# Attention and a gated MLP on one core: the softmax sums are kept, judged on the chip, and a second path stands behind a branch of GpSimd

## The chip, the cores and the metric

The kernel runs on one core of a Trainium2 chip. The core has a matrix engine (TensorE, PE in the profile, with its weight loads PEld), a vector engine (VectorE, DVE), a scalar engine (ScalarE, ACT), GpSimd (POOL) and SyncE (SP), which issues most transfers. The metric is the time of one execution on the device in microseconds (us); less is better. The kernel before takes 237.99 us, the median of three runs (237.53 to 238.32).

## What is computed

Eight batches, 384 tokens, 16 query heads on 4 key heads of 64 columns, a model width of 1024 and a gated MLP with 512 gated columns. Inputs and output are float32. Cut to what matters:

```python
scores = scale * np.matmul(q, k.transpose(0, 1, 3, 2))       # scale = 1/8
scores = scores - np.max(scores, axis=-1, keepdims=True)
attn = np.exp(scores)
attn = attn / (np.sum(attn, axis=-1, keepdims=True) + 1e-09)
x = np.matmul(attn, v)            # heads side by side: (8, 384, 1024)

h = np.maximum(x @ w_in, 0.0)     # (8, 384, 1024)
u, v = h[..., :512], h[..., 512:]
v_n = (v - mu) / np.sqrt(var + 1e-06)            # over the 512 columns
v_s = einsum('ts,bsd->btd', w_spatial, v_n) + b_spatial[None, :, None]
out = (u * v_s) @ w_out
```

The draws are small: `q`, `k` and `v` have a standard deviation of 0.1, so a score times its scale has one of about 0.01, each exponential is close to 1, and the sum of a query's 384 exponentials is close to 384.

## The kernel before

All matrix products are in float16 with float32 sums. The order of every engine's instructions is written out by hand: the kernel switches the scheduler off (line 51), and what the program issues first stands first in that engine's queue. A small planner in the kernel keeps a model clock of TensorE, ACT and DVE; `bank` (line 77) gives each product one of the eight PSUM banks, the one that by this model comes free first, and `spend` and `reads` (lines 85 and 88) advance the clock.

The attention of a batch is cut into 6 sets (3 tiles of 128 queries, 2 pairs of key heads). `units` (line 264) makes the scores, `exp` (line 288) the exponentials on ACT, with no maximum taken off first. `weigh` (line 292) multiplies them by the values. The values carry a column of ones, so each head's 65th column is the sum of its exponentials. DVE takes the reciprocal of four such columns into a small tile `r`, from a pool of four buffers (line 309), and multiplies by it:

```python
r = small.tile([P, G, 1], FP32, name=f"r_{b}_{s}_{hh}", tag="r")
reads(dve, 600.0, f"av_{b}_{s}_{hh}")
dve.reciprocal(r, o[:, :, D : D + 1])
```

That is done 96 times (8 batches, 6 sets, 2 halves), so 384 columns of `r` are made in all, and each is dead after its multiplication.

The MLP of a batch is a generator, `gated` (line 487), from which the attention's loop draws pieces of TensorE work. Of batch b it yields: `v_part` for three tiles of tokens (line 346; DVE takes the ReLU and the statistics), `u_part` for four blocks of columns (line 407; ReLU on ACT), and in the midst of these `root` (line 382, ACT) and `norm` (line 389: DVE makes `nmr`, POOL the three normalised tiles `vn`). Then, for each of four blocks, one output product of the batch before (`o_part`, line 456) and `s_part` (line 426: the product over tokens, then on DVE the sum `vs` with the bias, then on POOL the gate `gT`). The outputs of batch 7 come last, six calls of `o_part`, each copied by DVE or ACT and sent by SP or ACT. By then all attention is long done.

A program begins with a barrier of all engines that POOL opens, after four small memsets of constants; the profile has them at line 786. It ends with SP waiting for the transfers and engines one after the other, and two more barriers that POOL opens (line 797).

Of the kernel before, what the change touches and what calls it, by code (L numbers as in the profile page):

```python
# [1 line left out]

# [6 lines left out]

FP32 = mybir.dt.float32  # L10
FP16 = mybir.dt.float16
AF = mybir.ActivationFunctionType
ALU = mybir.AluOpType
PSUM = bass.MemoryType.PSUM
# [3 lines left out]
def kernel(  # L18
# [14 lines left out]
    nc = tc.nc  # L33
    P = 128
    B, HQ, S, D = q.shape
    HKV = k.shape[1]
    DM = moe_w_in.shape[0]
    DFF = moe_w_in.shape[1]
    DH = DFF // 2
# [3 lines left out]
    G = HQ // HKV  # L43
# [3 lines left out]
    SETS = 2 * NT  # L47
    UNITS = NT * SETS
    STEPS = UNITS // 2

    ctx.enter_context(tc.manual_schedule())

    cst = ctx.enter_context(tc.tile_pool(name="cst", bufs=1))
    ld = ctx.enter_context(tc.tile_pool(name="ld", bufs=2))
    att = ctx.enter_context(tc.tile_pool(name="att", bufs=2))
    moe = ctx.enter_context(tc.tile_pool(name="moe", bufs=2))
    small = ctx.enter_context(tc.tile_pool(name="small", bufs=4))
    ops = ctx.enter_context(tc.tile_pool(name="ops", bufs=3))
    ps = ctx.enter_context(tc.tile_pool(name="ps", bufs=1, space=PSUM))

    need = {AF.Exp, AF.Relu, AF.Copy, AF.Ln}
    set_id = next(
# [4 lines left out]
            name=nc.get_next_instruction_name(), act_func_set_id=set_id, ins=[], outs=[]  # L67
        )
    )
    pool, dve, act, sp = nc.gpsimd, nc.vector, nc.scalar, nc.sync  # L70
# [6 lines left out]
    def bank(shape, dtype, name):  # L77
        i = min(range(8), key=done.__getitem__)
        t = ps.tile(shape, dtype, name=name, tag=f"bank{i}")
        clock[nc.tensor] = max(clock[nc.tensor], done[i])  # L80
        done[i] = 1e12 + clock[nc.tensor]
        taken[name] = i
        return t

    def spend(ns):
        clock[nc.tensor] += ns

    def reads(eng, ns, name=None):
        clock[eng] = max(clock[eng], clock[nc.tensor] + 200.0) + ns
        if name:  # L90
            done[taken.pop(name)] = clock[eng]

    C512, C384, C128 = 216, 162, 56

    zero16 = cst.tile([P, P], FP16, name="zero16")
    dve.memset(zero16, 0.0)
# [54 lines left out]

    w_in16 = cst.tile([P, NK, DFF], FP16, name="w_in16")
    w_out16 = cst.tile([P, NM, DM], FP16, name="w_out16")
    wsT16 = cst.tile([P, NT, S], FP16, name="wsT16")
    bias_bc = cst.tile([P, S], FP32, name="bias_bc")
# [14 lines left out]

    ident16 = cst.tile([P, P], FP16, name="ident16")
    make_identity(nc, ident16)
    v1 = [cst.tile([P, HKV, NT, VW], FP16, name=f"v1_{i}") for i in range(2)]
    for i in range(2):
# [85 lines left out]


    aTs, x16s, xts = {}, {}, {}

    def units(u, count):
        b, r = divmod(u, UNITS)
        s, kt0 = divmod(r, NT)
        qt, j = divmod(s, 2)
        kts = range(kt0, kt0 + count)
        if kt0 == 0:
            aTs[b, s] = att.tile([P, NT, 2, G * P], FP16, name=f"aT_{b}_{s}", tag="aT", bufs=3)  # L270
        scs = [
            (kt, hh, bank([P, G * P], FP32, f"sc_{b}_{s}_{hh}_{kt}"))
            for hh in range(2)
            for kt in kts
        ]
        for kt, hh, sc in sorted(scs, key=lambda x: x[:2]):
            rows = slice(hh * D, (hh + 1) * D)
            nc.tensor.matmul(  # L278
                sc,
                kTs[b][rows, j, kt * P : (kt + 1) * P],  # L280
                qTs[b, j][rows, qt].rearrange("p (r i c) -> p i r c", r=G, i=G),
                start=True,
                stop=True,
            )
        spend(count * C512 + 186)
        return [(aTs[b, s][:, kt, hh], sc, f"sc_{b}_{s}_{hh}_{kt}") for kt, hh, sc in scs]

    def exp(a, sc, name):
        reads(act, 480.0, name)
        act.activation(a, sc, AF.Exp, scale=scale)  # L290

    def weigh(b, s, hh):
        qt, j = divmod(s, 2)
        aT = aTs[b, s]
        av = bank([P, 512], FP32, f"av_{b}_{s}_{hh}")
        for kt in range(NT):
            for i in range(G):
                nc.tensor.matmul(  # L298
                    av[:, i * (D + 1) : (i + 1) * (D + 1)],
                    aT[:, kt, hh, i * P : (i + 1) * P],  # L300
                    v1[b % 2][:, 2 * j + hh, kt, 0 : D + 1],
                    start=(kt == 0 and i == 0),
                    stop=(kt == NT - 1 and i == G - 1),
                )
        if s == 0 and hh == 0:
            x16s[b] = att.tile([P, NT, DM], FP16, name=f"x16_{b}", tag="x16")
        o = av[:, 0 : G * (D + 1)].rearrange("p (i d) -> p i d", i=G)
        spend(372)
        r = small.tile([P, G, 1], FP32, name=f"r_{b}_{s}_{hh}", tag="r")
        reads(dve, 600.0, f"av_{b}_{s}_{hh}")  # L310
        dve.reciprocal(r, o[:, :, D : D + 1])  # L311
        c = j * 512 + hh * 256
        dve.tensor_tensor(  # L313
            x16s[b][:, qt, c : c + 256].rearrange("p (i d) -> p i d", i=G),
            o[:, :, 0:D],
            r.to_broadcast([P, G, D]),
            ALU.mult,
        )
        measure()
# [62 lines left out]
    def root(b):  # L382
        measure()
        rstd = small.tile([P, NT], FP32, name=f"rstd_{b}", tag="rstd")
        act.activation(rstd, mvs[b][:, :, 1], AF.Ln, bias=eps_t)
        act.activation(rstd, rstd, AF.Exp, scale=-0.5)
        mvs[b, "rstd"] = rstd

    def norm(b):
        rstd = mvs[b, "rstd"]  # L390
        nmr = small.tile([P, NT], FP32, name=f"nmr_{b}", tag="nmr")
        dve.scalar_tensor_tensor(  # L392
            nmr, mvs[b][:, :, 0], -1.0, rstd, op0=ALU.mult, op1=ALU.mult
        )
        for st in range(NT):
            vn = moe.tile([P, DH], FP16, name=f"vn_{b}_{st}", tag="vn", bufs=6)
            (dve if b == 0 and st == 1 else pool).tensor_scalar(  # L397
                vn,
                v_r.pop((b, st)),
                rstd[:, st : st + 1],  # L400
                nmr[:, st : st + 1],
                op0=ALU.mult,
                op1=ALU.add,
            )
            v_n[b, st] = vn

    def u_part(b, m):
        if m == 0:
# [13 lines left out]
        reads(act, 400.0, f"pu_{b}_{m}")  # L422
        act.activation(uTs[b][:, m, :], pu[:, 0:S], AF.Relu)  # L423
        yield C384
# [62 lines left out]
    def gated():  # L487
        for b in range(B):
            u0 = b * UNITS
            behind = [(b - 1, tt, half) for tt in range(NT) for half in range(2)] if b else []  # L490
            if b == 0:
                for st in range(NT):
                    yield ("from", 6 * st + 7)
                    yield from v_part(b, st, 0, 4)
                    yield ("from", 6 * st + 10)
                    yield from v_part(b, st, 4, 8)
            else:
                yield ("from", u0 + 12)
                yield from v_part(b, 0)
                for _ in range(1 if b == B - 1 else 2):  # L500
                    yield from o_part(*behind.pop(0))
                yield ("from", u0 + 18)
                yield from v_part(b, 1)
                yield ("from", u0 + 24)
                yield from v_part(b, 2)
            for m in range(NM):
                i = 0
                for x in u_part(b, m):
                    yield x
                    i += 1  # L510
                    if (m, i) == (1, 6):
                        root(b)
                    if (m, i) == (2, 3):
                        norm(b)
            for m in range(NM):
                if behind:
                    yield from o_part(*behind.pop(0))
                yield from s_part(b, m)
            if behind:
                yield from o_part(*behind.pop(0))  # L520
        for tt in range(NT):
            for half in range(2):
                yield from o_part(B - 1, tt, half)
# [165 lines left out]
    total = UNITS * B  # L689
    ends = {}  # L690
    for i in range(SETS * B):
        ends.setdefault(NT * i + 4, []).append(divmod(i, SETS))
    fill = gated()
    wait_for = [0]

# [73 lines left out]
    wait_for[0] = 0  # L769
    pour(10**6, 1e12)  # L770
    assert not todo and not ends and next(fill, None) is None, (todo, ends)


# [28 lines left out]
```

## Time and profile before

| | us |
|---|---|
| median of three runs (lowest, highest) | 237.99 (237.53, 238.32) |
| span of the profiled execution | 236.4 (236.36 with one more digit) |
| median less span | 1.63 |
| busy in the span: PE, ACT, DVE, POOL | 230.1, 169.5, 142.7, 101.5 |
| PE busy between 216 and 231.8 us | all of it |

The span runs from the first instruction to the last of one profiled execution, so the metric holds a little more than it. An engine's busy time says how long instructions of its own ran. "Idle before" is time in which the engine stood still ahead of an instruction, and the arrow names what ended that wait. The granted TensorE clock is full (1.000) over the whole span. A row of the timeline is: start, duration, engine, line, operation, output and inputs, shape, count, and the idle time before it in brackets.

### The profile page before, as it was taken

The page shows a single profiled execution, that of the slowest core. Times are in us where ns is not written, and L with a number is a line of the kernel's source. Part 1 is how long each engine was busy: PE and PEld are TensorE (multiplying, and loading weights), DVE is VectorE, ACT ScalarE, POOL GpSimd, SP SyncE. Part 2 cuts the span into 40 slices and gives each one's busy share as a digit, 9 for nine tenths or more (in the row PEclk, how much of TensorE's full clock was granted, in tenths as well). Part 3 has the DMA queues.
Part 4 walks back from the last instruction along what each step waited for, and adds up shares of the span by engine and source line. Part 5 has one row for each costly group of instructions (what it writes and reads, how often), then busy time and mean ns, then how long its engine had stood idle before and what let it go on. Part 6 is the DMA issues. An engine that isn't in the chain of part 4 may idle for free.

```text
span 236.4 us, 5917 instructions
## 1 busy us (share of the span) xinstructions
PE 230.1 (97%) x2312; PEld 123.6 (52%) x2312; DVE 142.7 (60%) x379; ACT 169.5 (72%) x348; POOL 101.5 (43%) x145
## 2 busy tenths in 40 slices
PE   7899999999999999999999999999999999999993
PEld 6455655545554546544564545555465455545541
DVE  2568774676457764566646576376744667367362
ACT  2999989969997869977797776986697776401211
POOL 3669583651464543275045800575022500460550
PEclk9999999999999999999999999999999999999999
DMA  6999979999998999899989899389912643240147
GB/s 196 273 305 320 272 143 178 212 266 260 259 227 208 260 372 192 228 200 318 193 239 224 234 202 302 63 281 158 257 26 44 114 155 89 49 177 0 68 200 267
DMA packets 67467, 47.47 MB, mean 201 GB/s; under 512 B 48336, under 2 KB 60416, under 8 KB 67440
## 3 DMA queue, kind: packets, MB, share of 16 engines
q1 hardware_dynamic: 62512, 39.86, 69.4%
q0 software_dynamic: 3952, 6.42, 12.2%
q10 hardware_dynamic: 976, 0.82, 1.1%
q8 instruction: 18, 0.29, 0.5%
q14 instruction: 9, 0.07, 0.1%
HBM read 25.95 MB, written 12.58 MB: 163 GB/s over the span
## 4 chain that ended last, share of the span: by engine, by line
PE 93%; DVE 2%; DMA 2%; issue 0%; ACTq 0%; ACT 0%
PE pu L412 18%; PE pv L353 18%; PE po L469 18%; PE sc L278 15%; PE av L298 15%; PE psp L431 7%; DMA q<-in_q_dram 2%; PE qps L238 1%; PE xps L330 1%; DVE x L313 1%; DVE osb L216 1%; DVE qT L216 0%; DVE q L206 0%; DVE r L311 0%; DVE vr L367 0%
## 5 line engine op out<-in xcount | busy, mean ns | idle before, releaser
L290 ACT ACTIVATE aT<-sc 128x512 f16<-128x512 f32 x288 | 147.7, 612 | 31.0 <-PE sc L278 30.3
L298 PEld LDWEIGHTS <-aT 128*128 128x128 f16 x1152 | 47.0, 97 | 17.0 <-issue 2.1
L353 PE MATMUL pv<-w_in,xt 128*128 128x512 f16 x192 | 51.0, 380 | 0.1
L298 PE MATMUL av<-v,aT 128*128 128x65 f16 x1152 | 50.5, 193 | 0.0
L469 PE MATMUL po<-w_out,gT 128*128 128x512 f16 (+2 forms) x196 | 50.5, 375 | 0.0
L412 PE MATMUL pu<-xt,w_in 128*128 128x384 f16 x256 | 49.9, 326 | 0.0
L397 POOL TENSOR_SCALAR vn<-vr,rstd,nmr 128x512 f16<-128x512 f32 x23 | 17.7, 783 | 66.7 <-DVE nmr L392 45.3
L448 POOL TENSOR_TENSOR gT<-vs,uT 128x384 f16<-128x384 f32 x31 | 32.5, 1058 | 31.8 <-DVE r L311 16.9
L313 DVE TENSOR_TENSOR x<-av,r 128x256 f16<-128x256 f32 x96 | 40.7, 424 | 3.3
L278 PE MATMUL sc<-qT,kT 64*128 64x512 f16 x288 | 41.6, 380 | 0.4 <-DVE qT L216 0.2
L311 DVE RECIPROCAL r<-av 128x4 f32<-128x4 f32 x96 | 17.1, 179 | 40.4 <-PE av L298 40.1
L216 DVE COPY osb<-po 128x512 f32<-128x512 f32 (+1 forms) x39 | 26.6, 683 | 17.3 <-PE po L469 17.2
L412 PEld LDWEIGHTS <-w_in 128*128 128x128 f16 x256 | 22.1, 98 | 17.1 <-issue 5.5
L423 ACT ACTIVATE uT<-pu 128x384 f16<-128x384 f32 x32 | 15.8, 495 | 16.0 <-PE pu L412 15.8
L469 PEld LDWEIGHTS <-gT 128*128 128x128 f16 x196 | 17.4, 98 | 17.3 <-issue 3.2
L353 PEld LDWEIGHTS <-xt 128*128 128x128 f16 x192 | 15.8, 97 | 17.8 <-issue 6.0
L278 PEld LDWEIGHTS <-kT 64*128 64x128 f16 x288 | 10.9, 94 | 23.7 <-issue 12.1
L431 PE MATMUL psp<-wsT,vn 128*128 128x384 f16 x96 | 22.2, 327 | 0.0
L443 DVE TENSOR_TENSOR vs<-psp,bias_bc 128x384 f32<-128x384 f32 x32 | 17.6, 552 | 7.0 <-PE psp L431 6.9
L201 POOL CAST q<-q 128x768 f16<-128x768 f32 x22 | 17.6, 831 | 9.2 <-DMA q<-in_q_dram 4.5
L367 DVE TENSOR_SCALAR vr<-pv 128x512 f32<-128x512 f32 x24 | 16.4, 683 | 8.4 <-PE pv L353 8.3
L379 DVE BATCH_NORM_STATS2 stats<-vr 128x6 f32<-128x512 f32 x24 | 16.4, 685 | 0.1
(47 smaller groups left out, 98.9 us busy)
## 6 DMA issues: line engine op xcount, KB each, us to landing
out_dram<-osb SPq DMA_DIRECT2D x21, 512.0 KB, 3.2
q<-in_q_dram SPq DMA_DIRECT2D x10, 768.0 KB, 5.8
v_None<-in_v_dram SPq DMA_DIRECT2D x6, 384.0 KB, 5.8
w_in<-in_moe_w_in_dram POOLq DMA_DIRECT2D x4, 512.0 KB, 9.8
k_None<-in_k_dram SPq DMA_DIRECT2D x5, 384.0 KB, 4.0
q<-in_q_dram POOLq DMA_DIRECT2D x2, 768.0 KB, 8.4
out_dram<-osb SPq DMA_DIRECT2D x5, 256.0 KB, 2.2
w_out<-in_moe_w_out_dram POOLq DMA_DIRECT2D x2, 512.0 KB, 8.5
```

The lines of the kernel that those rows point to most:

```text
L201: eng.tensor_copy(t16[:, :, :, hh, :], src[:, hh])
L216: (act.copy if eng is act else dve.tensor_copy)(o, i)
L278: nc.tensor.matmul(sc, kTs[b][rows, j, kt * P : (kt + 1) * P], qTs[b, j][rows, qt].rearrange("p (r i c) -> p i r c", r=G, i=G), start=True ...
L290: act.activation(a, sc, AF.Exp, scale=scale)
L298: nc.tensor.matmul(av[:, i * (D + 1) : (i + 1) * (D + 1)], aT[:, kt, hh, i * P : (i + 1) * P], v1[b % 2][:, 2 * j + hh, kt, 0 : D + 1], st ...
L313: dve.tensor_tensor(x16s[b][:, qt, c : c + 256].rearrange("p (i d) -> p i d", i=G), o[:, :, 0:D], r.to_broadcast([P, G, D]), ALU.mult,)
L353: nc.tensor.matmul(pv, xts[b][:, kt, st * P : (st + 1) * P], w_in16[:, kt, DH:DFF], start=(kt == 0), stop=(kt == NK - 1),)
L397: (dve if b == 0 and st == 1 else pool).tensor_scalar(vn, v_r.pop((b, st)), rstd[:, st : st + 1], nmr[:, st : st + 1], op0=ALU.mult, op1=A ...
L412: nc.tensor.matmul(pu[:, 0:S], w_in16[:, kt, m * P : (m + 1) * P], xts[b][:, kt, :], start=(kt == 0), stop=(kt == NK - 1),)
L431: nc.tensor.matmul(psp[:, 0:S], v_n[b, st][:, m * P : (m + 1) * P], wsT16[:, st, :], start=(st == 0), stop=(st == NT - 1),)
L448: pool.tensor_tensor(gT, vs, uT, ALU.mult)
L469: nc.tensor.matmul(po[:, 0:width], gTs[b][:, m, tt * P : (tt + 1) * P], w_out16[:, m, c0 : c0 + width], start=(m == 0), stop=(m == NM - 1),)
```

## The change

The 96 small tiles `r` become slices of one tile `r_all` of 128 x 384 in the constant pool. It is never reused, so at the end it holds every reciprocal.

`judge` is called once, in the last batch, while `u_part` of its third block is under way. DVE reduces `r_all` over its 384 columns three times (maximum, minimum, sum). POOL fills `ones16` (128 x 128) and makes from the three values, in three instructions on 128 x 1, a float16 flag per partition: 1 if the minimum is above 0, the maximum at most 1 and the sum above 0, else 0.

`count` is called once, ahead of the third of the four last `s_part` blocks. TensorE multiplies the flags by the ones (one weight load and one product of one column, in a PSUM bank of its own), which gives the number of good partitions, and ACT copies it to SBUF.

After all else POOL loads that number into a register and compares it with the bits of 128.0. If it is another, POOL alone runs `with_maximum`, which computes the whole result again in float32, with each query's maximum, in loops, one instruction at a time, and overwrites the output. If it is 128.0, POOL jumps over that code. The other engines have no branch; SP waits for one more semaphore, which POOL sets on either way, before the last barriers. The code that is jumped over has some 1,020 instructions of POOL. In the built program four instructions that set registers of POOL also stand ahead of its four first memsets, before the opening barrier.

```diff
-    ctx.enter_context(tc.manual_schedule())
+    order = ctx.enter_context(ExitStack())
+    order.enter_context(tc.manual_schedule())
...
+    r_all = cst.tile([P, B * SETS * 2 * G], FP32, name="r_all")
...
-        r = small.tile([P, G, 1], FP32, name=f"r_{b}_{s}_{hh}", tag="r")
+        n = (b * SETS + s) * 2 + hh
+        r = r_all[:, n * G : (n + 1) * G].rearrange("p (i a) -> p i a", a=1)
...
+    ext = cst.tile([P, 3], FP32, name="ext")
+    fine16 = cst.tile([P, 1], FP16, name="fine16")
+    ones16 = cst.tile([P, P], FP16, name="ones16")
+    count32 = cst.tile([P, 1], FP32, name="count32")
+
+    def judge():
+        for i, op in enumerate((ALU.max, ALU.min, ALU.add)):
+            dve.tensor_reduce(ext[:, i : i + 1], r_all, axis=mybir.AxisListType.X, op=op)
+        pool.memset(ones16, 1.0)
+        pool.tensor_scalar(ext[:, 1:2], ext[:, 1:2], 0.0, None, op0=ALU.is_gt)
+        pool.tensor_scalar(ext[:, 0:1], ext[:, 0:1], 1.0, ext[:, 1:2], op0=ALU.is_le, op1=ALU.mult)
+        pool.tensor_scalar(fine16, ext[:, 2:3], 0.0, ext[:, 0:1], op0=ALU.is_gt, op1=ALU.mult)
+
+    def count():
+        pc = bank([P, 512], FP32, "count")
+        nc.tensor.matmul(pc[:, 0:1], ones16, fine16, start=True, stop=True)
+        spend(C128)
+        reads(act, 250.0, "count")
+        act.copy(count32, pc[:, 0:1])
...
+                    if (b, m, i) == (B - 1, 2, 5):
+                        judge()
             for m in range(NM):
+                if (b, m) == (B - 1, 2):
+                    count()
...
+    counted = pool.value_load(count32.bitcast(I32)[0:1, 0:1])
+    order.close()
+
+    with tc.If(counted != 0x43000000, preferred_fallthrough_block=False), ExitStack() as ctx:
+        again = ctx.enter_context(tc.tile_pool(name="again", bufs=1))
...
+        with tc.tile_critical():
+            with_maximum(nc, t, q, k, v, moe_w_in, moe_w_spatial, moe_b_spatial, moe_w_out, out)
...
+def with_maximum(nc, t, q, k, v, w_in, w_spatial, b_spatial, w_out, out):
+    g = OneByOne(nc.gpsimd)
...
+    with g.Fori(0, B, 1) as b:
+        with over(S, P) as t0:
+            with g.Fori(0, HKV, 1) as h:
+                move(
+                    qg.rearrange("p (r d) -> p r d", d=D),
+                    q[ds(b, 1), ds(h * G, G), ds(t0, P), :].rearrange("a r p d -> p (a r) d"),
+                )
+                with over(S, CK) as c:
+                    move(t["kv"], chunk(k, b, h, c))
+                    for r in range(G):
+                        g.tensor_tensor(
+                            prod, kv, qg[:, r * D : (r + 1) * D].rearrange("p (a d) -> p a d", a=1).to_broadcast([P, CK, D]), ALU.mult
+                        )
+                        fold(prod)
...
```

`OneByOne` follows every computing instruction of POOL with a wait until POOL is empty, `move` issues one transfer and waits for it, and `fold` halves an array by additions until one element is left.

## The prediction, as put on record

> **What bounds the kernel now.** I read the page's busy shares and slices first, then its chain of work that ended last, and then the timeline of the last 20 us, engine by engine, since everything the change adds (but for one spot at the start) lies there.
>
> ```profile
> span 236.4 us, 5917 instructions
> PE 230.1 (97%) x2312; PEld 123.6 (52%) x2312; DVE 142.7 (60%) x379; ACT 169.5 (72%) x348; POOL 101.5 (43%) x145
> PE   7899999999999999999999999999999999999993
> ...
> PE 93%; DVE 2%; DMA 2%; issue 0%; ACTq 0%; ACT 0%
> PE pu L412 18%; PE pv L353 18%; PE po L469 18%; PE sc L278 15%; PE av L298 15%; PE psp L431 7%; DMA q<-in_q_dram 2%; PE qps L238 1%; PE xps L330 1%; DVE x L313 1%; DVE osb L216 1%; DVE qT L216 0%; DVE q L206 0%; DVE r L311 0%; DVE vr L367 0%
> ```
>
> The reader is to see one bound from beginning to end: 93% of the chain is TensorE, in matrix products alone, and no engine that waits for it costs anything. So an addition counts only if it is a TensorE instruction, if it makes TensorE wait, or if it lies before its first or after its last product. How much the others may do without being seen, the timelines of the last stage tell, first DVE, then POOL, then ACT:
>
> ```profile
> 218.30 0.16 DVE L392 SCALAR_TENSOR_TENSOR nmr<-mv,rstd 128x3 f32<-128x3 f32 x1 [0.67 <-ACT rstd L386]
> 222.06 0.69 DVE L216 COPY osb<-po 128x512 f32<-128x512 f32 x1 [3.60 <-PE po L469]
> ```
>
> ```profile
> 218.67 2.28 POOL L397 TENSOR_SCALAR vn<-vr,rstd,nmr 128x512 f16<-128x512 f32 x3 [6.84 <-PE pu L412]
> 223.30 1.06 POOL L448 TENSOR_TENSOR gT<-vs,uT 128x384 f16<-128x384 f32 x1 [2.35 <-DVE vs L443]
> 224.71 1.07 POOL L448 TENSOR_TENSOR gT<-vs,uT 128x384 f16<-128x384 f32 x1 [0.35 <-DVE vs L443]
> 226.02 1.06 POOL L448 TENSOR_TENSOR gT<-vs,uT 128x384 f16<-128x384 f32 x1 [0.24 <-DVE vs L443]
> 227.41 0.88 POOL L451 TENSOR_TENSOR gT<-vs,uT 128x256 f16<-128x256 f32 x1 [0.33 <-DVE vs L443]
> ```
>
> ```profile
> 221.20 0.49 ACT L423 ACTIVATE uT<-pu 128x384 f16<-128x384 f32 x1 [0.81 <-PE pu L412]
> 224.76 0.59 ACT L216 COPY osb<-po 128x512 f32<-128x512 f32 x1 [3.07 <-PE po L469]
> ```
>
> To be seen: after `nmr` DVE stands still for 3.60 us, after the third `vn` (at 220.95) POOL for 2.35 us, after the last `uT` ACT for 3.07 us, and POOL has nothing at all to do after 228.29 (227.41 + 0.88). TensorE in this stage has no gap: by the busy time in windows it is busy for 5.00 of the 5 us from 216 to 221 and for all 5.40 of 221 to 226.4 and of 226.4 to 231.8.
>
> **Part 1: the sums are kept.** 96 reciprocals write 128x4 into another tile, with the same instruction, input and size; the reader of each is the next DVE instruction, as before. Nothing is added to any queue; in the built program DVE's order differs by the three reductions alone. Cost 0.
>
> **Part 2: `judge` on DVE.** Three reductions of 128x384 float32. The trace has none. Rows near to it: the smallest DVE row with floats, `nmr` on 128x3, 0.16 us; statistics over 128x512 (BATCH_NORM_STATS2, line 379), 0.685 us; the sum `vs` over 128x384, 0.552 us. So three take between 0.5 and 2.1 us. I take 0.5 each (384 of the 512 columns of the statistics), 1.5 us. They stand right behind `nmr` (ends 218.46) and ahead of the copy `osb` at 222.06, in 3.60 us of idle time, with even 2.1 us over by 220.6. Nothing is queued behind them that is ready earlier. Cost 0; without that cover 1.5 us of DVE would hold the copy and then a PSUM bank.
>
> **Part 3: `judge` on POOL.** A memset of 128x128 float16 and three instructions on 128x1, behind the third `vn`, ahead of the first `gT`. The same memset stands at the start of the program with 0.205 us. For 128x1: a memset of that shape is 0.10 us, `vn`, the same kind of instruction on 512 columns, is 0.77. I take 0.2 each for they are 512 times narrower but read two operands; 0.8 us in all, 0.5 to 2.5 by the bounds. DVE's values are there by 220.0 (at most 220.6), before POOL is, so no wait for DVE is added. POOL is done at 220.95 + 0.8 = 221.75 (at most 223.46); `gT` is to start at 223.30, for `vs` is not ready before. Cost 0, at the upper end 0.16 us of `gT`, which the 0.35, 0.24 and 0.33 us of idle time ahead of the next three swallow.
>
> **Part 4: `count`.** One weight load and one product of one column, behind the second `psp` of the last batch, which ends at 223.86 (timeline of PE: start 223.21, 0.65). It waits for POOL's flags, there since 221.75 (at most 223.46), so by no bound of the rows does TensorE wait. The price of the pair itself: a product of `av` has 65 columns and its own weight load; 1152 of them make 14.6% of the chain, 34.5 us, or 30 ns each. The row of the group itself shows 193 ns for one, as latency, and 97 ns for its weight load; were the pipe drained for it, that would be 0.29 us. I take two `av` steps, **0.06 us**, from 0.03 to 0.29. The eight banks are dealt out anew behind `count`; each bank's reader before is one or two us done when the next product needs it (the tightest: the second `po` of batch 7 takes the bank of `count` itself, free three us earlier). ACT's copy of one column costs between 0.20 (128x3, line 386) and 0.27 us (the copy of 128x128), from about 224.1 to 224.4, in the idle 3.07 us that end at 224.76. Cost 0.
>
> **Part 5: the start.** Four register instructions of POOL before its first memsets, and POOL opens the first barrier:
>
> ```profile
> 0.24 0.10 POOL L786 MEMSET const-float32-0.0<- 128x1 f32 x1 [0.24 <-issue]
> 0.28 0.10 POOL L786 MEMSET const-float32-1.0<- 128x1 f32 x1
> 0.31 0.10 POOL L786 MEMSET const-bfloat16-1.0<- 128x1 bf16 x1
> 0.34 0.10 POOL L786 MEMSET const-uint8-127<- 128x1 uint8 x1
> 0.73 0.20 POOL masks.py:197 MEMSET ident<- 128x128 f16 x1 [0.29 <-POOLq L786]
> 0.74 0.39 SPq L112 DMA_DIRECT2D k_None<-in_k_dram  x1
> ```
>
> The memsets follow each other every 0.035 us, and the first load is issued at 0.74, after POOL. The trace has one MOVE of POOL, 39 ns; four are **0.16 us**, from 0 (POOL came to its first instruction early) to 0.4 (0.1 each, as a memset). All of it delays the whole program.
>
> **Part 6: the end of POOL.** A register is loaded from SBUF, compared, two semaphores are passed, and POOL jumps over some 1,020 instructions to the closing block. It may last until SP has its last transfer:
>
> ```profile
> 229.05 4.30 SPq L482 DMA_DIRECT2D out_dram<-osb  x6
> ...
> 232.95 0.37 ACTq L482 DMA_DIRECT2D out_dram<-osb  x1
> ```
>
> SP's last issue ends at 233.35, having begun at 233.02, and a 192 KB output takes 2.3 us to land by the page: 235.3. POOL is free from 228.3, so **the cover is 7.0 us**. The load is not in the trace; it lies between that MOVE (0.04) and a whole transfer out of SBUF (the 64 KB output of ACT lands in 1.9), and I take 1.9, the safe end. The code behind the jump has to be fetched. How long instruction transfers are, the page shows:
>
> ```profile
> q8 instruction: 18, 0.29, 0.5%
> q14 instruction: 9, 0.07, 0.1%
> ```
>
> 0.5% of 16 engines' 236.4 us is 18.9 us, by 18 is 1.05 us for 16 KB; in queue 14 it is 0.4 us for 8 KB. With the way to and from memory I take 2.4 us, what the first load of the program needs for 96 KB from issue to landing. 1.9 + 2.4 = 4.3 us, hidden with 2.7 to spare. SP's additional wait (some 0.03 to 0.07 us) stands ahead of the last landing. Cost 0.
>
> **Sum.** 0.06 + 0.16 = 0.22 us; by the bounds 0.03 to 0.69 (0.29 + 0.4). The profiled span of 236.36 becomes 236.6. The median of the runs is 1.63 us above that span, which I keep: 236.36 + 0.22 + 1.63 = 238.21, **238.2 us**, 0.1% more than 237.99.
>
> **Rivals.**
>
> *POOL outlasts its cover (slower).* The place is the jump after 228.3. For it: a jump over 1,020 instructions has no like in this trace, and each piece of code is a transfer. Against it: 7.0 us are three such transfers. From 7.0 us on, each further us is a us of the span. With three fetches one after the other (behind the comparison, at the target, and behind that) it would be 1.9 + 3 x 2.4 = 9.1 us, 2.1 late: 240.3 us. The Trainium skill, Runtime: NRT & Kernel Launch, section Instruction fetch mechanics, speaks for it: code is prefetched only in sequence, and a taken branch to a page that isn't held must fetch it before going on. By that rule the stall is sure and only its length is open; no row of this trace shows one. The skill's DMA: Bandwidth & Descriptors, Latency and other measured facts, puts a register load at a floor of some 0.6 us; with that the end is an estimated 1.3 us shorter than with my 1.9, and the sum is the same.
>
> *TensorE waits for the flags (slower).* If POOL's small instructions cost as much as `gT` (1.06 us) each, with the memset they end at 220.95 + 0.2 + 3.2 = 224.3, and TensorE, ready at 223.86, stands still for 0.5 us: 238.7 us, on the border of what can be told. `gT` then starts 1.0 late, of which 0.9 is taken up by its idle times. Against it: `vn` over 512 columns takes only 0.77.
>
> *The check fails and the second path runs.* Its innermost loop alone has 8 x 3 x 4 x 24 = 2304 passes with a transfer of about 2 us, 5 ms. Sums near 384 have reciprocals near 0.0026, inside of 0 to 1; this I hold to be excluded but for an error in the flags.
>
> *Nothing can be seen at all, or less time* : only if the start and TensorE's pair cost nothing, 238.0; no row offers a gain, for TensorE has no wait in this stage that could go.
>
> **Chances.** My forecast (with its own bounds, 238.0 to 238.7) 0.78; POOL's end 0.10; TensorE's wait 0.06; the second path 0.01; something not listed 0.05. About 0.3%, 0.7 us, is what a measurement of this kernel can tell from no change. Of the forecast's 0.78 I put 0.73 within that, 0.03 above and 0.02 below (the runs shown spread by 0.8 us); half of the wait's and some of the rest lie within too. Faster 0.03, within 0.78, slower 0.19. The range: 237.7, as the runs scatter below 238.0, to 239.2, which takes in the bounds, the wait, and an overrun of up to 1 us.
>
> **What would show it.** In the profile after: three reductions between 218.5 and 220.6; POOL's small ones done before 223.3; no wait of PE for POOL at the product of `count`; the first load issued near 0.9 instead of 0.74; SP's closing waits held by transfers and not by POOL. Wrong it would be if SP's or the barrier's last wait is for POOL, if PE shows a wait behind `count`, or if the time between the span and the median is not 1.6 us any more.

## The result, and the profile after

The changed kernel takes 239.31 us (median of 22 runs, 238.71 to 240.93); the kernel before, run beside it 22 times, takes 238.47. The ratio is 1.0039, with a 95% interval of 1.0021 to 1.0056: slower by 0.9 us, where 0.2 was forecast, and just above the forecast range (237.7 to 239.2). The median span of the changed kernel is 237.45 us; its profiled execution has 237.12 us, against 236.36.

The added work itself went as laid out. From the timelines of the changed kernel, DVE, POOL, PE and ACT in turn (start, duration, engine, line, what):

```profile
218.39 0.16 DVE L396 SCALAR_TENSOR_TENSOR nmr<-mv,rstd 128x3 f32<-128x3 f32 x1 [0.67 <-ACT rstd L390]
218.47 1.47 DVE L420 TENSOR_REDUCE ext<-r_all 128x1 f32<-128x384 f32 x3
222.15 0.69 DVE L218 COPY osb<-po 128x512 f32<-128x512 f32 x1 [2.22 <-PE po L495]
```

```profile
220.97 0.20 POOL L421 MEMSET ones<- 128x128 f16 x1
221.14 0.24 POOL L422 TENSOR_SCALAR ext<-ext 128x1 f32<-128x1 f32 x1
221.49 0.31 POOL L423 TENSOR_SCALAR ext<-ext 128x1 f32<-128x1 f32 x1
221.90 0.30 POOL L424 TENSOR_SCALAR fine<-ext 128x1 f16<-128x1 f32 x1
223.40 1.05 POOL L474 TENSOR_TENSOR gT<-vs,uT 128x384 f16<-128x384 f32 x1 [1.20 <-DVE vs L469]
```

```profile
223.79 0.17 PE L428 MATMUL count<-fine,ones 128*128 128x1 f16 x1
223.82 1.02 PE L495 MATMUL po<-w_out,gT 128*128 128x512 f16 x4
```

```profile
224.03 0.16 ACT L431 COPY count<-count 128x1 f32<-128x1 f32 x1 [2.25 <-PE count L428]
```

The reader is to see that the work of DVE, POOL and ACT lies in idle time: DVE still waits 2.22 us for TensorE afterwards, POOL 1.20 for `vs`, and TensorE goes from the start of `count` to the next product in 0.03 us. Laid side by side, the products of the two traces keep their distance up to here (0.09 to 0.12 us from 60 us on), and behind `count` it is 0.025 us larger.

The start is later. The first constant and the first load of the changed kernel:

```profile
0.49 0.10 POOL L1023 MEMSET const-float32-0.0<- 128x1 f32 x1 [0.49 <-issue]
...
0.97 0.40 SPq L114 DMA_DIRECT2D k_None<-in_k_dram  x1
```

0.97 instead of 0.74: the four register instructions (MOVE) stand at 0.20, 0.27, 0.33 and 0.39, 0.06 apart.

The rest is at the end. TensorE's last product starts 0.12 us later than before, the last issue of an output ends 0.12 later (233.47 against 233.35), but the last output packet ends at 235.73 instead of 234.98. So from the last issue to the last packet it is 2.27 us instead of 1.63. The list of transfers has it too; queue 14 in it carries code. Before, with size and median time to landing:

```profile
q14 instruction: 9, 0.07, 0.1%
...
out_dram<-osb SPq DMA_DIRECT2D x5, 256.0 KB, 2.2
...
out_dram<-osb SPq DMA_DIRECT2D x1, 192.0 KB, 2.3
...
out_dram<-osb ACTq DMA_DIRECT2D x1, 64.0 KB, 1.9
```

After:

```profile
q14 instruction: 11, 0.09, 0.1%
...
out_dram<-osb SPq DMA_DIRECT2D x5, 256.0 KB, 3.1
...
out_dram<-osb SPq DMA_DIRECT2D x1, 192.0 KB, 2.9
...
out_dram<-osb ACTq DMA_DIRECT2D x1, 64.0 KB, 2.7
```

Every output of batch 7 lands later, and queue 14 has two more packets of code. The two that come after the jump are 8 KB each, begin at 230.44 and 233.25 and take 0.31 us each in the trace. POOL's records beside them (start, duration in us):

```
227.52  0.49   TENSOR_LOAD      the count into a register
228.07  0.04   COMPARE_BRANCH
228.62  0.04   COMPARE_BRANCH   the jump over the second path
230.44  0.31   code, 8 KB
232.02  1.21   DRAIN            first instruction of the closing block
233.25  0.31   code, 8 KB
236.36  0.02   EVENT_SEMAPHORE  the last barrier, behind SP
```

The first row starts while POOL's last `gT` (227.53, 0.88 us) is still running. The jump takes 3.40 us and POOL is ready at 233.2, 3.1 us ahead of SP: its time is hidden. Its packets are not. In windows over the end of the kernel before (span, PE, PEld, DVE, ACT, POOL busy, TensorE clock, DMA share, GB/s) the DMA engines are full while the outputs leave:

```profile
226.00:229.00 3.00, 3.00 (x17) 1.33 (x16) 2.78 (x5) 0.00 (x0) 1.94 (x2) 1.00 0.43 175
229.00:232.00 3.00, 3.00 (x16) 1.46 (x15) 0.93 (x3) 1.17 (x2) 0.00 (x0) 1.00 0.95 365
232.00:234.00 2.00, 0.62 (x7) 0.31 (x5) 0.99 (x2) 0.27 (x1) 0.00 (x0) 1.00 0.97 361
```

A share of 0.95 and 0.97 means that the 16 engines have hardly a pause in which one of them could catch up. Output packets that begin later than 2.00 us after the start of the last issue: none before; after, 12 of them, up to 2.59. Before, the last packet ends 1.96 us after that start. After, two packets at once are last seen at 1.92 (before, at 1.91); from there to 2.60 there is never more than one under way, each beginning as the one before it ends. So a single one of the 16 engines trails, by 0.64 us, close to two times 0.31. It is so in every other run that had code packets among the outputs. The trace doesn't number the engines; that the one which trails is the one that fetched the code is inferred from this sum.

### The profile page after: what moved, and what is told of

Read it like the earlier page. It is cut to its first block, busy times and chain, and to the rows that moved or that the text cites. A ratio compares the mean times of both kernels' runs of the same rounds, so it can differ in the third digit from the quotient of the medians.

```text
span 237.1 us, 5939 instructions
## 1 busy us (share of the span) xinstructions
PE 230.1 (97%) x2313; PEld 123.7 (52%) x2313; DVE 144.0 (61%) x382; ACT 169.3 (71%) x349; POOL 102.1 (43%) x149
## 4 chain that ended last, share of the span: by engine, by line
PE 86%; DMA 6%; DVE 2%; SPq 1%; POOL 1%; issue 0%; ACTq 0%; ACT 0%
PE pu L438 17%; PE po L495 17%; PE pv L357 17%; PE sc L281 14%; PE av L301 13%; PE psp L457 6%; DMA q<-in_q_dram 4%; DMA qT<-q 2%; SPq L258 1%; PE qps L240 1%; POOL vn L401 1%; PE xps L334 1%; DVE x L317 1%; DVE qT L218 1%; DVE osb L218 1%; POOL q L206 0%
## 5 line engine op out<-in xcount | busy, mean ns | idle before, releaser
L317 DVE TENSOR_TENSOR x<-av,r_all 128x256 f16<-128x256 f32 x96 | 40.8, 424 | 3.3
L315 DVE RECIPROCAL r_all<-av 128x4 f32<-128x4 f32 x96 | 17.1, 179 | 40.5 <-PE av L301 40.1
```

The source lines that it names most:

```text
L317: dve.tensor_tensor(x16s[b][:, qt, c : c + 256].rearrange("p (i d) -> p i d", i=G), o[:, :, 0:D], r.to_broadcast([P, G, D]), ALU.mult,)
```

## The experiments

Theory A, at first: the branch and its code cost the time. Theory B: the judging does. From the first four runs came theory C: the code behind a far jump comes in two packets while the outputs hold all DMA engines, and what shares an engine with them lands late, by their own duration. Its rival is that the landing follows from the long jump as such. The table has the first load in us from the start, the number of instructions jumped over (1041 in the changed kernel, the "some 1,020" of the text above), the jump from the branch to the next instruction of POOL, the code packets between the jump and the last output packet, and the time from the end of the last issue to the end of the last output packet. These are read from one profiled execution each. Rows without a ratio were executed once, so that their total time tells little:

| run | first load | instructions jumped over | jump | code packets | issue to last packet | ratio to before (95%) |
|---|---|---|---|---|---|---|
| before | 0.74 | none | none | 0 | 1.63 | |
| changed | 0.97 | 1041 | 3.40 | 2 | 2.27 | 1.0039 (1.0021 to 1.0056) |
| e1_again | 0.97 | 1041 | 3.38 | 2 | 2.35 | 1.0048 (1.0020 to 1.0077) |
| e14_again | 0.97 | 1041 | 3.40 | 2 | 2.26 | 1.0026 (0.9997 to 1.0055) |
| e2_no_branch | 0.72 | none | none | 0 | 1.62 | 1.0000 (0.9974 to 1.0027) |
| e3_small_body | 0.72 | 37 | 0.16 | 0 | 1.63 | 0.9987 (0.9963 to 1.0010) |
| e6_body130 | 0.72 | 133 | 0.45 | 1 | 1.84 | |
| e7_body300 | 0.72 | 293 | 3.40 | 2 | 2.32 | |
| e4_long_body | 0.72 | 1049 | 3.38 | 2 | 2.23 | 1.0019 (0.9998 to 1.0040) |
| e8_late | 0.97 | 1041 | 2.63 | 1, at the very end | 1.61 | |
| e5_hint | 0.96 | 1041 | 0.50 | 2 | 2.34 | 1.0038 (1.0011 to 1.0064) |
| e12_hint_pad | 0.97 | 1105 | 0.50 | 2 | 2.34 | |
| e13_hint_late | 0.96 | 1041 | 0.51 | 2 | 2.36 | 1.0044 (1.0014 to 1.0074) |
| e9_few_before | 0.73 | none | none | 0 | 1.61 | |
| e10_few_after | 0.97 | 1041 | 2.83 | 2 | 1.85 | |
| e11_small_moves | 0.85 | few | 0.16 | 0 | 1.63 | |

**The changed kernel again**, twice. 

> The changed kernel once more, so that the others have it on the same chip. It should be 0.5 to 1.4 us above the kernel before, with the first load issued at 0.97 us and the time less the span near 1.9 us (1.65 before). If the last outputs' landing, 0.6 us later in the first profile, belongs to the change, the last landing is again 2.9 us or more after the last issue; if it is scatter of transfers, it falls between 2.2 and 2.9.

> The changed kernel beside it on the same chip: 0.6 to 1.2 us above before, last packet 2.25 to 2.35 us after the last issue, two packets of code between the jump and the end.

239.45 against 238.40 and 239.26 against 238.56. The late landing is there each time, so it is no scatter of transfers. (The interval of e14_again just takes in no change.) The time less the span is 1.93 and 1.97 us, against 2.02 and 2.03 for the kernel before: nothing is lost outside of the span. The 1.9 that I had expected there as a sign of loss was none, because before has as much.

**No branch.**

```diff
-    counted = pool.value_load(count32.bitcast(I32)[0:1, 0:1])
     order.close()
-    with tc.If(counted != 0x43000000, preferred_fallthrough_block=False), ExitStack() as ctx:
...
```

> Sums kept, judged and counted, but the number is never loaded, and there is no branch and no second path (the output isn't guarded any more). Theory A, the branch and its code cost the time (register instructions ahead of the barrier, code fetched behind the jump): 0 to 0.15 us above before, first load at 0.74, time less span 1.65. Theory B, the judging costs it (TensorE's pair, the copies): 0.6 us or more above before. The product of count itself moves TensorE by 0.03 us in either.

Two of the three signs of theory A came: ratio 1.0000 and first load at 0.72. The third, a time less span of 1.65, did not: it is 2.07, but the kernel before has 2.02 itself, so that sign was set by a wrong number. The landing is as before. Theory B falls: judging and counting stay in, move TensorE by 0.025 us, and cost nothing else that the trace shows; the interval of the time alone reaches up to the 0.6 us of theory B.

**The second path short, and long without the register instructions.**

```diff
-            with_maximum(nc, t, q, k, v, moe_w_in, moe_w_spatial, moe_b_spatial, moe_w_out, out)
+            for _ in range(510):          # 4 in e3, 52 in e6, 132 in e7
+                nc.gpsimd.memset(t["one"], 0.0)
+                nc.gpsimd.drain()
```

> The same with the load and the branch, but the second path is four memsets (its computation is left out), so that POOL jumps over 37 instructions instead of 1041, and there are no register instructions at the start. Theory A with the length of the jump as cause: as without a branch, 0 to 0.15 us above before, time less span 1.65. Theory A with any taken jump as cause: time less span 1.9, 0.3 to 0.45 above before. Theory B: 0.6 or more.

> The second path is 510 memsets, each with a wait until POOL is empty (its computation is left out): POOL jumps over 1049 instructions as in the changed kernel, but without register instructions at the start. Theory A: first load at 0.74, time less span 1.9, two more packets of code at the end as in the changed kernel; 0.3 us above before, and 0.2 to 0.6 below the changed kernel. Theory B: as the changed kernel.

> The second path is 52 memsets (its computation is left out): POOL jumps over 133 instructions, 8.3 KB. Theory C: the landing follows the number of code packets between the jump and the end, 1.62 us after the last issue for none, 1.93 for one, 2.25 for two; I expect one.

> The second path is 132 memsets (its computation is left out): POOL jumps over 293 instructions, 18 KB. Theory C: two packets and 2.25 us from the last issue to the last landing, a jump of 3.4 us as with 1041 instructions, for it is the fetch and not the distance that takes the time.

A jump over 37 instructions takes 0.16 us, brings no packet and costs nothing that can be told. Over 133 it brings one packet and the landing is 0.21 later (0.31 was expected), over 293 two and 0.69, over 1049 two and 0.60: it goes by the packets, not by the number of instructions. 293 cost as much as 1049, in the jump too. In this series a long jump and two packets still come together; the runs below part them. The time of e4 is 0.78 us above before between the medians and 0.45 by the ratio, whose interval just takes in no change; 0.3 had been expected. The time less the span is 2.2 us in e3 and e4, above the kernel before's 2.02 and above all that was expected of them; no run shows why. The outputs of batch 7 in the runs with 37, 133 and 1049 (count, size, median us to landing), one line of each list of transfers:

```profile
out_dram<-osb SPq DMA_DIRECT2D x5, 256.0 KB, 2.3
```

```profile
out_dram<-osb SPq DMA_DIRECT2D x5, 256.0 KB, 2.7
```

```profile
out_dram<-osb SPq DMA_DIRECT2D x5, 256.0 KB, 3.1
```

That is 0.4 us in this median for each packet that the jump brings.

**The jump after the outputs.**

```diff
+    pool.tensor_copy(ext[:, 0:1], osbs[B - 1, NT - 1][:, 383:384])
+    pool.tensor_copy(ext[:, 1:2], osbs[B - 1, NT - 1][:, 1023:1024])
     counted = pool.value_load(count32.bitcast(I32)[0:1, 0:1])
```

> The changed kernel, but POOL copies two numbers of the last output tile before it loads the count, so that it jumps only after the last copy, near 234 us, and its code comes when the outputs have nearly landed. Theory C: the last landing comes back to 1.6 us after the last issue. The rival (a long jump as such delays the landing): 2.25 again. In both, the jump is no longer covered: POOL comes to the last barrier at about 233.1 + 0.5 (copies) + 0.9 (load, branch) + 3.4 + 1.2 = 239.1 us instead of 236.4, so that the span is some 2 to 3 us longer than the changed kernel's.

This tells theory C from its rival: the jump is long (2.63 us), the first packet comes at 234.94, just before the last output packet ends (234.96), and the landing is back at 1.61. What it costs is in SP's waits from 233 us on (for whom: us in total, times, longest):

```profile
SPq L1036 <- PEq L1036: 2.9, 2, 2.4
SPq L1036 <- DMA out_dram<-osb: 1.6, 4, 0.8
```

In the changed kernel:

```profile
SPq L1034 <- DMA out_dram<-osb: 2.1, 4, 0.9
SPq L1034 <- PEq L1034: 0.7, 2, 0.5
```

The wait for outputs falls from 2.1 to 1.6 us, but now SP waits 2.4 at the barrier that POOL opens. (The row names PE, which passes that barrier with it.) This is the rival that I had named in the prediction, and it shows its price: POOL comes to the barrier at 237.85, 2.3 us behind SP. It costs that only because the jump was put 5 us later. The span is 1.5 us longer than the changed kernel's, where 2 to 3 had been expected: the jump was 2.63 us instead of 3.4.

**A hint to the sequencer**, alone, with a longer second path, and with the late jump.

```diff
+    tc.mark_branch_hint_location("again", hint="LikelyTaken", engines=[pool.engine])
...
-    with tc.If(counted != 0x43000000, preferred_fallthrough_block=False), ExitStack() as ctx:
+    with tc.If(counted != 0x43000000, preferred_fallthrough_block=True, label="again"), ExitStack() as ctx:
```

> The changed kernel with the block order turned (POOL's compare itself jumps to the closing block) and a hint to POOL's sequencer, early in its queue, that this jump will be taken. Theory C, formed from the first four runs: the code behind the jump comes in two packets of 8 KB, 0.31 us each, while the last outputs keep all 16 DMA engines busy, and the one engine that carries them finishes 0.62 us later, and the last output with it. If the hint brings the code before the outputs, the last packet lands 1.6 us after the last issue instead of 2.25 and the jump takes under 1 us; the time is 0.2 to 0.4 us above before instead of 0.9. If the hint does nothing: 2.25 us, a jump of 3.4 us, 0.9 above before. The rival to theory C, that the landing follows POOL's long jump by itself, expects 2.25 whenever the jump is long.

> The kernel with the hint, and 64 more instructions in the second path that isn't run, which moves the closing code by half of a block of 8 KB. If the second packet of code is there because the closing code crosses a block, the number of packets in the output's time changes from two to one, and the last packet lands 1.93 us after the last issue instead of 2.34; if each jump takes two in any case, nothing changes.

> The hint and the late jump together, the second path whole: the jump is short, for the code at its target is held (0.6 us with the hint against 3.4), and comes so late that the packets which follow it find the outputs landed. If theory C is all of the loss at the end: last packet 1.6 us after the last issue, POOL at the last barrier near 235.4 us and so not later than SP, and what is left against before is the start (0.25) and TensorE's pair (0.03): 0.1 to 0.5 us above before, 0.3 to 0.9 below the changed kernel. If POOL is late by more than I reckon, the span is longer by that.

The jump falls from 3.4 to 0.5 us, so the hint works; yet the time is as without the hint, 1.0038. That separates the two once more: after a short jump with two packets among the outputs (229.88 and 235.17) the last output lands late, 2.34. Moving the closing code by 64 instructions changed nothing; so, for this one distance, there is no sign that the second packet is there for a block's border.

The hint also has a price of its own. In all three kernels with it, and in no other, TensorE waits 0.3 us in batch 6 for the last normalised tile of POOL, whose first starts 0.3 us later than without the hint, and from there on TensorE is 0.30 us behind. From e5_hint:

```profile
206.29 0.34 PE L457 MATMUL psp<-wsT,vn 128*128 128x384 f16 x1 [0.29 <-POOL vn L401]
```

No run shows why POOL is late there. So the times of e5 and e13 hold this too, and are no measure of the packets alone.

The late jump with the hint was a miss: I had reckoned its packets to come behind the outputs, and they came at 235.53 and 235.98, while the last output packet ended at 236.85, 2.36 after the issue. Without the delay it would have ended near 236.1. It takes nothing off the changed kernel. The branch as such can be had without the loss, as e3 shows; but no version was found that takes it off with the whole second path in place.

**Pauses for the DMA engines.**

```diff
-            elif half:
+            elif half and b < B - 2:
                 sp.dma_start(rows[:, tt, :], osb)
```

> The kernel before without the output transfers of batch 6 (that part of the output is left out), so that the 16 DMA engines have pauses in the last microseconds. Pair of the next run: from the last issue to the last packet 1.3 to 1.6 us.

> The changed kernel without the output transfers of batch 6 (that part of the output is left out). Theory C: the first code packet, over two us before the last issue, is caught up in the pauses, the second, at about the last issue, still costs 0.3 us: the last landing is 0 to 0.35 us later after the last issue than in its pair, instead of 0.65. The rival (a long jump as such delays the landing): 0.65 again.

With batch 6 not written, two packets cost 0.24 us (1.85 against 1.61) instead of 0.64, after a jump of 2.83 us. The DMA share is 0.57 to 0.84 in each microsecond from 230 to 234, against 0.93 to 1.02 in the changed kernel, and 0.99 in the microsecond after. So the first packet, at 230.05, finds pauses between the outputs to be caught up in, and the second, at 233.25, hardly any. The collision needs full engines: theory C.

**Two register instructions.**

```diff
-            with_maximum(nc, t, q, k, v, moe_w_in, moe_w_spatial, moe_b_spatial, moe_w_out, out)
+            with nc.gpsimd.Fori(0, B, 1) as i:
+                nc.gpsimd.dma_start(
+                    t["x"], out[bass.ds(i, 1), 0:P, :].rearrange("a p f -> p (a f)")
+                ).then_inc(t["sem"], 16)
...
```

> The second path is a loop with one transfer at a changing address (its computation is left out): two register instructions of POOL stand ahead of the first barrier instead of four, and the jump is short. If each costs its 0.06 us there, the first load is issued at 0.84 us (0.72 with none, 0.97 with four), and the last packet lands 1.62 us after the last issue.

0.85 us, between 0.72 and 0.97: 0.06 for each. The last packet lands 1.63 us after the last issue, as expected.

## Why the prediction was wrong

- **The step that failed is part 6, "Cost 0".** That POOL's time is hidden was right, but its sum came close by luck: I had put 1.9 for the register and 2.4 for the code, and they took 0.49 and 3.40, and the DRAIN of 1.21 us behind the jump was not in it at all. POOL was ready at 233.2, only 0.6 later than by my sum, as its load did not wait for the last `gT`; that 3.1 us were to spare, where I had 2.7, comes from SP, which was itself held up by the late outputs. What failed is that I took the code for a latency of POOL alone and not for traffic. I had read the price of a packet off queue 14 (0.4 us; 0.31 in the trace) and had the DMA row of the page before me, and didn't ask what leaves by the same engines between 228 and 235 us: the outputs, on which the end hangs. Two packets make 0.62, and the landing is 0.64 later. It falls under "something not listed", which had 0.05.
- **Part 5, the start, was mis-sized**: 0.23 to 0.25 instead of 0.16. I had multiplied the duration of a MOVE (0.039); what counts is the distance of one from the next, 0.06. It lay within the bounds. This is the first load alone; whether as much reaches the end isn't shown (below).
- **Part 4, TensorE**: 0.025 instead of 0.06 (bounds 0.03 to 0.29), no wait. Parts 1 to 3 cost nothing, as said: DVE's reductions took 1.47 us (1.5 said), POOL's three instructions 0.24 to 0.31 each (0.2 said) and end at 222.20, 1.6 us ahead of TensorE.
- **The sum**: 0.24 + 0.025 + 0.64 = 0.9 us, and the three comparisons with the changed kernel give 0.84, 1.05 and 0.70 between the medians. That this adds up is no proof of each part. The 0.64 and the 0.025 stand in the traces. That the 0.24 of the start reaches the end isn't shown: the last product of TensorE is only 0.12 later in the profiled pair, and the first 17 us scatter by more than that; e4, without the register instructions, is 0.27 below the changed kernel beside it (239.18 against 239.45), which the scatter of the runs doesn't set apart from nothing.
- **The anchor was low.** Three runs gave 237.99, 22 gave 238.47; the time less the span is 2.02 us (median of 35 runs, none under 1.96), not 1.63, the median of three less the span of one profiled execution. Of the 1.1 us between 238.21 and 239.31, 0.48 are this; the other 0.62 are what the change cost beyond the forecast 0.22, about what the packets explain. Without the packets, the result would have lain inside the range in spite of the low anchor.
- **The rivals.** POOL did not outlast its cover, and TensorE did not wait for the flags. The rule of the Trainium skill (Runtime: NRT & Kernel Launch, Instruction fetch mechanics), that a taken branch to code that isn't held waits for its fetch, is borne out by the 3.40 us; the way in which it cost time here, on the queues of others, was in none of my rivals. For the register load the Trainium skill (DMA: Bandwidth & Descriptors, Latency and other measured facts) has a floor of about 0.6 us; the trace has 0.49, and the measurement decides.

## What to carry to other kernels

A far jump is a transfer: besides how long its own engine stands still, ask what is on the DMA engines at that moment, and what ends last on them. Here, where outputs filled all engines at the end, the last landing was 0.21 us later for one packet of code of 8 KB and 0.60 to 0.75 for two. A second path that is never run still cost by where its jump lay, and its instructions put the first load up to 0.25 us later; one of some 40 instructions, without such instructions, cost nothing that could be told.

## What the runs showed of the hardware

- POOL's jump: 0.16 us over 37 instructions, 0.45 over 133, 3.38 to 3.40 over 293, 1041 or 1049, but 2.63 and 2.83 over 1041 in e8 and e10, where the outputs had left or had pauses; 0.50 over 1041 with the hint. The compare itself takes 0.04 us (0.07 with the hint).
- Entering the closing block after the branch, POOL needs a DRAIN of 1.13 to 1.21 us. In the kernel before it is 2.06, as it starts beside the last `gT`, and it ends 1.16 after that.
- The first 17 us, in which the engines wait for the first loads, scatter by over a microsecond from one execution to the next: against the kernel before, TensorE was at 17 us between 0.51 us early (e12_hint_pad) and 1.00 late (e2_no_branch). From 60 us on, every trace keeps its distance to within 0.03 us, but for `count` and for the 0.30 us in the kernels with the hint.
